# The last two raw weight chunks are converted inside the hand-over from attention to the expert, and VectorE splits the first weights

## The chip, the cores and the metric

One Trainium2 core runs the whole program. The metric is the device time in microseconds (us). The engines are TensorE (PE in the profile, with its weight loads as PEld), VectorE (DVE), ScalarE (ACT), GpSimd (POOL) and SyncE (SP), which issues every transfer of this kernel from one queue, in program order.

## The reference, cut to what matters

```python
scores = scale * q @ k.T                    # 4 batches x 12 heads, 448 tokens, head size 64
attn = softmax(where(mask, -1e9, scores)) @ v
x = attn.transpose(0, 2, 1, 3).reshape(1792, 768)
h = x @ w_in                                # w_in 768 x 2048, 64-bit floats in memory
P = a0 + a1*h + a2*h**2 + a3*h**3
Q = 1 + |b0|*|h| + |b1|*h**2
out = (P / (Q + 1e-6)) @ w_out              # w_out 2048 x 768, 64-bit floats in memory
```

## The kernel before, in words

**Attention.** The 48 heads are worked as 24 pairs, numbered p = 0 to 23. One pass of the loop over p is written out by hand in the string `ORDER`: each word is a task, and `@n` says for which pair it runs (`c.1@2` in pass p is the transposes of pair p-2). In a pass, TensorE transposes q and k (`psA`), multiplies scores (`psS`), transposes the normalized exponentials (`psC`) and multiplies with v (`psD`). VectorE adds the mask and takes the maxima (L329), ScalarE takes the exponentials (L339), GpSimd adds up the sums (`sm`, L346), VectorE inverts them (`r`, L349), GpSimd multiplies seven tiles by them (`n`, L353), and VectorE and ScalarE copy the transposes out of PSUM (`v`, `a`).

**Weights.** Each of the 32 blocks of 128 rows or columns of the weights ("chunk" m) arrives as 64-bit words (`raw`, 768 KB, `conv_load`) and is turned into 32-bit floats in steps: step 1 and step 5 are one GpSimd multiply each (L162, L166), step 2 and step 3 are one VectorE shift-and-or each (L172, L178), and the result (384 KB) is stored to memory (`conv_store`). There are three `raw` buffers, so chunk m+3 can be loaded when chunk m is done. The first ten chunks are converted in the attention passes: `quota(p)` says how many of the 20 half-chunks pass p takes. In the expert part each 32-bit block is loaded again (`load_w`, tag `ld`, three buffers used in turn) and split into a high part (`w_hi`, a rounding copy) and a low part (`w_lo`, a subtraction); a first-use block of `w_out` is stored split (L218).

**Expert.** Unit t is a block of 128 hidden features for 512 tokens: `p1(t)` are 18 products into `psH`, then a chain over ScalarE and VectorE (`act_a`, `dve_a`, `act_b`, `dve_b`) gives g, which is split into `gh` (ScalarE) and `gl`; `p2(t)` are 24 products into `psO` and `psM`.

**The hand-over.** After pass 23 the string `TAIL` orders the last attention tasks among the first expert tasks (`p1.0` to `p1.2`, `p2.0`); then a loop runs units t = 2 and on. Three facts of the code matter below. SP issues in program order, so a load that waits for a free `ld` buffer holds all behind it. `lw.4.0` takes the buffer that `wl.0.1` frees, `lw.2.1` the one that `wl.3.0` frees. And in the loop ScalarE makes `w_hi(2, 1)`, which reads what `lw.2.1` loaded, before its part `act_b(2)` of the chain:

```python
            if not late:
                split_w(t, 1)
            ...
            act_b(t)
```

In the names of the rows, `whl` is a split weight, `w` a 32-bit weight (or a scratch tile of the chain), `u` the scratch of a conversion (or of the chain).

Of the kernel before, what the change touches and what calls it, by code (L numbers as in the profile page):

```python
# [32 lines left out]
THIRD = "qk@-1 qy@-1 qx@-1" + ORDER.replace("qk@-1", "").replace(" qy@-1", "").replace(" qx@-1", "")  # L33

TAIL = """
c.1@2 e.6@1 c.0@2 e.0@1 v.1@2 dh@3 a.1@2 sm@1 v.0@2 a.0@2 r@1 dl@3 n.2@1 n.3@1 xr n.5@1 n.0@1 wh.1.0 p1.0 n.4@1
n.6@1 d@2 n.1@1 wl.1.0 c.1@1 c.0@1 co aa.0 da.0 dh@2 dl@2 a.1@1 v.1@1 dz.0 a.0@1 v.0@1 p1.1 wh.2.0 ab.0 wl.2.0 db.0 d@1 dy.0
lw.4.0 gh.0 gl.0 wh.0.1 wl.0.1 aa.1 da.1 p1.2 xl dh@1 dl@1 dz.1 ab.1 wh.1.1 wl.1.1 wh.3.0 lw.2.1 xa.10 p2.0
lw.3.1 aa.2 lw.5.0 db.1 wl.3.0 dy.1 wh.4.0 wl.4.0
"""  # L40

# [17 lines left out]
def kernel(  # L59
# [11 lines left out]
    nc = tc.nc  # L71
# [9 lines left out]
    NP = B * HP  # L81
# [18 lines left out]
    ab = const.tile([P, 6], F32, name="ab")  # L100
# [10 lines left out]
    xs = {  # L111
        (ck, part, kh): xp.tile([P, K3, 512], F32R, tag=f"x{ck}{part}{kh}", name="xs")
        for ck in range(2) for part in range(2) for kh in range(2)
    }
    x_raw = [xp.tile([P, K3, 2 * NT], F32, name=f"xr{kh}") for kh in range(2)]
    xr = {(kh, tk): x_raw[kh][:, :, tk * NT:(tk + 1) * NT] for kh in range(2) for tk in range(2)}
# [14 lines left out]
    def splits(t, n):  # L131


        return n == 0 or n_use[t] == 0
# [5 lines left out]
    def conv_load(m):  # L140
        if m >= len(items):
            return
        f, n = items[m]
        raw = c_raw[m] = cv.tile([P, DM, 2], U32, tag="raw", bufs=NR, name="raw64")
        if n == 0:
            nc.sync.dma_start(
                out=raw.rearrange("p (c f) t -> p c (f t)", c=KD),
                in_=moe_w_in[:, f * P:(f + 1) * P].bitcast(U32).rearrange("(c p) f -> p c f", p=P),
            )
        else:  # L150
            nc.sync.dma_start(
                out=raw.rearrange("p m t -> p (m t)"), in_=moe_w_out[f * P:(f + 1) * P, :].bitcast(U32)
            )

    def conv_step(m, s):
        raw = c_raw[m]
        yu = raw[:, :, 1]
        y = yu.bitcast(F32)
        if s == 1:
            pool, tag, bufs = (lv, f"u{m}", 1) if NL <= m < NC - 3 else (cv, "u", 3)  # L160
            u = c_u[m] = pool.tile([P, DM], U32, tag=tag, bufs=bufs, name="u")
            nc.gpsimd.tensor_scalar(  # L162
                out=u.bitcast(F32), in0=y, scalar1=0.0, scalar2=1.0, op0=ALU.mult, op1=ALU.mult
            )
        elif s == 5:
            nc.gpsimd.tensor_scalar(  # L166
                out=y, in0=y, scalar1=2.0 ** -112, scalar2=1.0, op0=ALU.mult, op1=ALU.mult
            )
        elif s == 4:
            nc.scalar.activation(out=y, in_=y, func=AF.Copy, scale=2.0 ** -112)  # L170
        elif s == 2:
            nc.vector.scalar_tensor_tensor(  # L172
                out=c_u[m], in0=raw[:, :, 0], scalar=29, in1=c_u[m],
                op0=ALU.logical_shift_right, op1=ALU.bitwise_or,
            )
        else:
            o = cv.tile([P, DM], F32, tag="ld", bufs=NL, name="w").bitcast(U32) if m < NL else c_u[m]
            nc.vector.scalar_tensor_tensor(  # L178
                out=o, in0=yu, scalar=3, in1=c_u[m], op0=ALU.logical_shift_left, op1=ALU.bitwise_or
            )  # L180
            c_32[m] = o.bitcast(F32)

    def conv_store(m):
        nc.sync.dma_start(out=w32[items[m]], in_=c_32[m])
        stored.add(items[m])

    def load_w(t, n):
        if t >= len(w_units) or (n_use[t] == 0 and (w_units[t][1], n) in items[:NL]):
            return
        f = w_units[t][1]  # L190
        if not splits(t, n):
            x = int(t < NPL + KF - 1 or (t - NPL - KF + 1) % 5 > 1)
            w = wp.tile([P, 2, DM], F32R, tag=f"w{x}", bufs=NWB[x], name="whl")
            nc.sync.dma_start(out=w.bitcast(F32), in_=w_hl[f, n])
            w_split[t, n] = (w[:, 0], w[:, 1])
        elif (f, n) in stored:
            w = cv.tile([P, DM], F32, tag="ld", bufs=NL, name="w")
            nc.sync.dma_start(out=w, in_=w32[f, n])
            w_raw[t, n] = w

    def w_hi(t, n):
        if not splits(t, n):
            return

        src = w_raw.pop((t, n)) if (t, n) in w_raw else c_32[items.index((w_units[t][1], n))]
        w = wp.tile([P, 2, DM], F32R, tag=f"w{n}", bufs=NWB[n], name="whl")
        nc.scalar.copy(out=w[:, 0], in_=src)
        w_split[t, n] = (w, src)

    def w_lo(t, n):  # L210
        if not splits(t, n):
            return
        w, src = w_split[t, n]
        eng = nc.gpsimd if t < 3 or n == 1 else nc.vector
        eng.tensor_tensor(out=w[:, 1], in0=src, in1=w[:, 0].bitcast(F32), op=ALU.subtract)  # L215
        w_split[t, n] = (w[:, 0], w[:, 1])
        if n == 1:
            nc.sync.dma_start(out=w_hl[w_units[t][1], n], in_=w.bitcast(F32))  # L218

    def split_w(t, n):  # L220
        w_hi(t, n)
        w_lo(t, n)
# [43 lines left out]
    def half(j):  # L266
        return slice(j * D, (j + 1) * D)
# [158 lines left out]
                nc.vector.tensor_copy(out=o, in_=ps[:, r])  # L426

    def quota(p):
        return int(3 <= p < NP - 1)

    steps = [(m, n) for m in range(NC) for n in (2, 3)]
    done = []
# [1 line left out]
    def conv(p, part):  # L434
        if part == 0:
            lo = sum(quota(x) for x in range(p))
            for m, n in steps[lo:lo + quota(p)]:
                conv_step(m, 1 if n == 2 else 5)
        elif part == 3:
            while done:  # L440
                conv_load(done.pop(0) + NR)
        else:
            lo = sum(quota(x) for x in range(p))
            mid, hi = lo + quota(p) // 2, lo + quota(p)
            for m, n in steps[lo:mid] if part == 1 else steps[mid:hi]:
                conv_step(m, n)
                if n == 3:
                    done.append(m)
# [391 lines left out]
    def coeffs():  # L840
        nc.sync.dma_start(out=ab[:, 0:4], in_=moe_a.partition_broadcast(P))
        nc.sync.dma_start(out=ab[:, 4:6], in_=moe_b.partition_broadcast(P))

    def coeffs_done():
# [4 lines left out]
    tasks.update({  # L849
        "co": coeffs_done, "xr": close_r, "xl": close_l, "p1": p1, "p2": p2, "aa": act_a, "da": dve_a, "dz": dve_a3,  # L850
        "ab": act_b, "db": dve_b, "dy": dve_b3, "gh": g_hi, "gl": g_lo, "wh": w_hi, "wl": w_lo,
        "lw": load_w, "xa": lambda m: conv_step(m, 1), "xs": conv_store, "xd": conv_load,
    })

    def evict_now():
# [24 lines left out]
    with tc.manual_schedule():  # L880
# [9 lines left out]
        sm = es_l.enter_context(pool(name="sm", bufs=4))  # L890
# [10 lines left out]
        for x in range(2):  # L901
            m = mask[half(x), S - QB:]
            nc.gpsimd.affine_select(
                out=m, in_=m, compare_op=ALU.is_ge, fill=-1e9 / SCALE, base=0, pattern=[[-1, QB]], channel_multiplier=1,
# [29 lines left out]
        def attend(p, part):  # L934
            for fn, arg, lag in part:
                if 0 <= p - lag < NP:
                    fn(p - lag, *arg)

        for p in range(NHEAD, NP):
            if p == 20:  # L940
                coeffs()
            if p in (1, 2, 3):
                conv_load((1, 2, 3).index(p))
            attend(p, begin[p] if 0 <= p < 3 else plan)
            for m in {20: (3, 0), 21: (4, 1, 5), 22: (6, 2, 7), 23: (8, 9)}.get(p, ()):
                conv_store(m)
            if p == NP - 2:
                split_w(0, 0)
            if p == NP - 2:
                load_w(0, 1)  # L950
            if p == NP - 1:
                load_w(3, 0)
                load_w(1, 1)
# [61 lines left out]
        for j in range(HF):  # L1015
            n = j + 5
# [46 lines left out]
```

## Time and profile before

| what | value |
|---|---|
| device time, median of 3 runs | 606.29 us (605.68 to 607.68) |
| the profiled execution's own time | 605.96 us |
| its span | 604.2 us |
| busy share of the span: PE, DVE, ACT, POOL | 98%, 88%, 74%, 30% |
| bytes moved | 131.00 MB, mean 217 GB/s |

The span is from the first to the last instruction; 1.76 us lie around it. Times in rows are counted from the span's start. A busy engine is one with an instruction in flight, which on VectorE and GpSimd holds time in which the instruction only stands; the idle time in brackets is that in front of an instruction, with what ended it.

### The profile page before, as it was taken

What the parts mean: (1) busy time and instruction counts of PE and PEld (TensorE: products, weight loads), DVE (VectorE), ACT (ScalarE), POOL (GpSimd) and SP (SyncE); (2) the same over time, 40 slices, a digit from 0 to 9 for tenths busy, and PEclk for the clock granted to TensorE, in tenths of its full rate; (3) what the DMA queues carried; (4) which work ended last, traced back from release to release, by engine and by line L of the source; (5) the groups of instructions that cost most, each with busy time, mean ns of one, the idle gap of its engine ahead of it and who ended that gap; (6) DMA issues with size and microseconds to landing.
All of it is one profiled execution on the core that took longest, in us unless ns stands there. A gap on an engine that the chain in (4) does not pass through costs nothing.

```text
span 604.2 us, 12764 instructions
## 1 busy us (share of the span) xinstructions
PE 594.9 (98%) x4660; PEld 494.6 (82%) x4660; DVE 534.7 (88%) x1013; ACT 446.4 (74%) x917; POOL 180.1 (30%) x274
## 2 busy tenths in 40 slices
PE   8999999999999999999999999999999999999997
PEld 6666666667788888888888888889999999998886
DVE  3999999985789999999999879998999999988950
ACT  4999999997687766777877776675486777677731
POOL 2899999886535311221333100000000000000000
PEclk9999999999999999999999999999999999999999
DMA  7979889788569988888985664433363343259872
GB/s 164 218 185 224 196 206 208 168 248 292 187 237 319 324 307 312 307 304 303 351 311 184 219 231 153 158 131 131 116 221 119 122 156 135 75 177 347 293 251 81
DMA packets 105727, 131.00 MB, mean 217 GB/s; under 512 B 70592, under 2 KB 83008, under 8 KB 105664
## 3 DMA queue, kind: packets, MB, share of 16 engines
q1 hardware_dynamic: 105664, 130.18, 68.0%
q8 instruction: 37, 0.61, 0.4%
q14 instruction: 26, 0.21, 0.1%
HBM read 99.49 MB, written 30.67 MB: 215 GB/s over the span
## 4 chain that ended last, share of the span: by engine, by line
PE 69%; DVE 15%; ACT 7%; issue 4%; POOL 4%; DMA 1%; SPq 0%; DVEq 0%; POOLq 0%; ACTq 0%
PE psO L601 22%; PE psH L232 17%; PE psQ L715 14%; PE psM L597 12%; ACT e L339 4%; DVE psS L329 4%; POOL e L353 3%; DVE at L384 3%; DVE u L172 2%; ACT at L382 1%; PE psS L318 1%; POOL whl L215 1%; PE psI L930 1%; DVE nm L329 1%; PE psC L372 1%
## 5 line engine op out<-in xcount | busy, mean ns | idle before, releaser
L601 PE MATMUL psO<-whl,gh 128*128 128x512 f32 x448 | 159.4, 392 | 0.3 <-ACT gh L527 0.2
L232 PE MATMUL psH<-xs,whl 128*128 128x512 f32 x576 | 136.7, 391 | 0.2 <-ACT e L339 0.2
L597 PE MATMUL psM<-whl,gh 128*128 128x256 f32 x448 | 126.3, 282 | 0.0
L232 PEld LDWEIGHTS psH<-xs,whl 128*128 128x128 f32 x576 | 106.0, 188 | 21.8 <-ACT e L339 0.3
L601 PEld LDWEIGHTS psO<-whl,gh 128*128 128x128 f32 x448 | 84.0, 188 | 18.7 <-ACT gh L527 1.5
L597 PEld LDWEIGHTS psM<-whl,gh 128*128 128x128 f32 x448 | 84.7, 189 | 1.6 <-DVE osb L585 0.3
L339 ACT ACTIVATE e<-psS,nm 128x448 f32<-128x448 f32 (+6 forms) x168 | 79.4, 571 | 5.8 <-DVE nm L329 3.7
L353 POOL TENSOR_SCALAR e<-e,r 128x192 f32<-128x192 f32 (+6 forms) x168 | 79.0, 492 | 11.4 <-DVE r L349 8.3
L601 PE MATMUL psO<-whl,gl 128*128 128x512 f32 x224 | 81.1, 391 | 0.0
L715 PE MATMUL psQ<-xpart,wq 128*128 128x384 f32 x432 | 78.5, 337 | 0.1
L715 PEld LDWEIGHTS psQ<-xpart,wq 128*128 128x128 f32 x432 | 74.7, 188 | 1.5 <-DVE hpair L741 0.4
L329 DVE CUSTOM_DVE_ANT_0 psS<-psS,mask 128x64 f32<-128x64 f32 (+6 forms) x168 | 65.5, 461 | 2.0 <-PE psS L318 1.3
L597 PE MATMUL psM<-whl,gl 128*128 128x256 f32 x224 | 63.2, 282 | 0.0
L162 POOL TENSOR_SCALAR u<-raw 128x768 f32<-128x768 f32 x32 | 39.2, 1226 | 53.8 <-DMA raw<-in_moe_w_out_dram 16.3
L318 PE MATMUL psS<-qkt 64*64 64x64 f32 (+6 forms) x672 | 47.5, 391 | 1.8 <-ACT e L339 1.6
L601 PEld LDWEIGHTS psO<-whl,gl 128*128 128x128 f32 x224 | 42.0, 188 | 8.8
L339 ACT ACTIVATION_READ_ACCUMULATOR e<-psS,nm 128x1 f32 x168 | 49.0, 303 | 0.0
L504 ACT ACTIVATE w<-w 128x512 f32<-128x512 f32 x32 | 20.2, 633 | 38.4 <-DVE w L489 38.3
L396 PE MATMUL psD<-at,vraw 128*64 128x448 f32 (+3 forms) x384 | 46.8, 386 | 0.4 <-issue 0.4
L396 PEld LDWEIGHTS psD<-at,vraw 128*64 128x64 f32 x384 | 25.6, 136 | 25.2 <-issue 14.7
L597 PEld LDWEIGHTS psM<-whl,gl 128*128 128x128 f32 x224 | 42.4, 189 | 0.0
L318 PEld LDWEIGHTS psS<-qkt 64*64 64x64 f32 x672 | 21.4, 132 | 20.8 <-ACT at L382 10.1
(109 smaller groups left out, 1119.2 us busy)
## 6 DMA issues: line engine op xcount, KB each, us to landing
whl<-whl SPq DMA_DIRECT2D x64, 768.0 KB, 5.3
w<-w SPq DMA_DIRECT2D x54, 384.0 KB, 5.0
raw<-in_moe_w_in_dram SPq DMA_DIRECT2D x16, 768.0 KB, 6.1
raw<-in_moe_w_out_dram SPq DMA_DIRECT2D x16, 768.0 KB, 5.6
w<-u SPq DMA_DIRECT2D x29, 384.0 KB, 3.1
qraw<-in_q_dram SPq DMA_DIRECT2D x48, 112.0 KB, 3.9
kraw<-in_k_dram SPq DMA_DIRECT2D x48, 112.0 KB, 3.9
out_dram<-osb SPq DMA_DIRECT2D x13, 384.0 KB, 3.1
```

Source lines behind the costliest of these rows:

```text
L162: nc.gpsimd.tensor_scalar(out=u.bitcast(F32), in0=y, scalar1=0.0, scalar2=1.0, op0=ALU.mult, op1=ALU.mult)
L232: nc.tensor.matmul(ps, w[:, c * P:(c + 1) * P], xs[ck, part, c // K3][:, c % K3], start=(c == 0 and n == 0), stop=(c == KD - 1 and n == 2),)
L318: nc.tensor.matmul(pss[p, b][half((1 + b + j) % 2)], QK[p][half(j), 0, b * QB:(b + 1) * QB], QK[p][half(j), 1, :b_w[b]], start=True, stop= ...
L329: nc.vector.tensor_tensor_reduce(out=s, in0=s, in1=mask[:, S - w:], scale=-SCALE, scalar=3e38, op0=ALU.add, op1=ALU.min, accum_out=nmx[p][ ...
L339: nc.scalar.activation(out=E[p % 2][i][:, :w], in_=pss[p, i], func=AF.Exp, bias=nmx[p][:, i:i + 1], scale=-1.0, accum_out=SUM[p % 2][:, i: ...
L353: nc.gpsimd.tensor_scalar(out=e, in0=e, scalar1=REC[p][:, i:i + 1], scalar2=0.0, op0=ALU.mult, op1=ALU.add)
L384: nc.vector.tensor_copy(out=o, in_=i)
L396: nc.tensor.matmul(ps[half(j), lo * QB:S], v[:, j, c], a[h][:, slot * QB:(slot + 7 - lo) * QB], start=(c == 0), stop=(c == 3), skip_group_ ...
L504: nc.scalar.activation(out=w, in_=w, func=AF.Abs)
L597: nc.tensor.matmul(acc["m", k], g, w[:, 512:], start=first and (k % 2 == 0 or each), stop=last, skip_group_check=True)
L601: nc.tensor.matmul(acc[k], g, w[:, :512], start=first, stop=last)
L715: nc.tensor.matmul(q_bank[j, bank], w[:, wp_, c * P:(c + 1) * P], xp_[:, c], start=(first and n == 0), stop=(n == 3 * K3 - 1), skip_group_ ...
```

## The change

Chunks 8 and 9 leave passes 19 to 22 (`quota` ends four passes sooner) and their steps, stores and the loads of chunks 11 and 12 are written into `TAIL`. The stores of pass 23 go with them. The split of unit 0's two blocks leaves ScalarE: both high parts become a VectorE copy, and the low part of the first block becomes a VectorE subtraction that stands in `TAIL` as `wl.0.0` (it was a GpSimd subtraction in pass 22). The coefficients' task `co` stands earlier.

```diff
 TAIL = """
-c.1@2 e.6@1 c.0@2 e.0@1 v.1@2 dh@3 a.1@2 sm@1 v.0@2 a.0@2 r@1 dl@3 n.2@1 n.3@1 xr n.5@1 n.0@1 wh.1.0 p1.0 n.4@1
-n.6@1 d@2 n.1@1 wl.1.0 c.1@1 c.0@1 co aa.0 da.0 dh@2 dl@2 a.1@1 v.1@1 dz.0 a.0@1 v.0@1 p1.1 wh.2.0 ab.0 wl.2.0 db.0 d@1 dy.0
-lw.4.0 gh.0 gl.0 wh.0.1 wl.0.1 aa.1 da.1 p1.2 xl dh@1 dl@1 dz.1 ab.1 wh.1.1 wl.1.1 wh.3.0 lw.2.1 xa.10 p2.0
+c.1@2 e.6@1 c.0@2 e.0@1 v.1@2 dh@3 a.1@2 xa.8 sm@1 xa.9 v.0@2 a.0@2 r@1 wl.0.0 co
+xc.8.2 xc.9.2 dl@3 n.2@1 n.3@1 xr n.5@1 n.0@1 wh.1.0 p1.0 n.4@1
+n.6@1 d@2 n.1@1 xc.8.5 xc.9.5 wl.1.0 c.1@1 c.0@1 aa.0 da.0 dh@2 dl@2 a.1@1 v.1@1 dz.0 a.0@1 v.0@1 xc.8.3 xs.8 xd.11
+p1.1 wh.2.0 ab.0 wl.2.0 db.0 d@1 dy.0
+lw.4.0 xc.9.3 xs.9 xd.12 gh.0 gl.0 wh.0.1 wl.0.1 aa.1 da.1 p1.2 xl dh@1 dl@1 dz.1 ab.1 wh.1.1 wl.1.1 wh.3.0 lw.2.1 xa.10 p2.0
 lw.3.1 aa.2 lw.5.0 db.1 wl.3.0 dy.1 wh.4.0 wl.4.0
 """
...
-        nc.scalar.copy(out=w[:, 0], in_=src)
+        if t:
+            nc.scalar.copy(out=w[:, 0], in_=src)
+        else:
+            nc.vector.tensor_copy(out=w[:, 0], in_=src)
...
-        eng = nc.gpsimd if t < 3 or n == 1 else nc.vector
+        eng = nc.gpsimd if 0 < t < 3 or n == 1 else nc.vector
...
     def quota(p):
-        return int(3 <= p < NP - 1)
+        return int(3 <= p < NP - 5)
...
-        "lw": load_w, "xa": lambda m: conv_step(m, 1), "xs": conv_store, "xd": conv_load,
+        "lw": load_w, "xa": lambda m: conv_step(m, 1), "xc": conv_step, "xs": conv_store, "xd": conv_load,
...
-            for m in {20: (3, 0), 21: (4, 1, 5), 22: (6, 2, 7), 23: (8, 9)}.get(p, ()):
+            for m in {20: (3, 0), 21: (4, 1, 5), 22: (6, 2, 7)}.get(p, ()):
                 conv_store(m)
             if p == NP - 2:
-                split_w(0, 0)
-            if p == NP - 2:
+                w_hi(0, 0)
                 load_w(0, 1)
```

On SP, from the end of pass 22 into the hand-over, before (`raw_3224` is chunk 12, `w_5_0` and `w_3_1` are the stores of chunks 8 and 9, `w<-w_4_0` is `lw.4.0`, `w<-w_2_1` is `lw.2.1`):

```order
119 L198 DMA w<-w_0_1_84 128x768
120 L146 DMA raw_3224<-in_moe_w_in_dram 128x6x256
121 L184 DMA w_5_0_93<-u 128x768
122 L184 DMA w_3_1_90<-u 128x768
123 L198 DMA w<-w_3_0_89 128x768
124 L198 DMA w<-w_1_1_86 128x768
125 L198 DMA w<-w_4_0_91 128x768
126 L218 DMA whl_1_115<-whl 128x1536
127 L218 DMA whl_1_116<-whl 128x1536
128 L198 DMA w<-w_2_1_88 128x768
```

The same place on SP in the change (`raw_3434` is now chunk 11, `raw_3477` chunk 12):

```order
118 L200 DMA w<-w_0_1_84 128x768
119 L200 DMA w<-w_3_0_89 128x768
120 L200 DMA w<-w_1_1_86 128x768
121 L186 DMA w_5_0_93<-u 128x768
122 L153 DMA raw_3434<-in_moe_w_out_dram 128x1536
123 L200 DMA w<-w_4_0_91 128x768
124 L186 DMA w_3_1_90<-u 128x768
125 L148 DMA raw_3477<-in_moe_w_in_dram 128x6x256
126 L223 DMA whl_1_115<-whl 128x1536
127 L223 DMA whl_1_116<-whl 128x1536
128 L200 DMA w<-w_2_1_88 128x768
```

Two stores and two loads of raw chunks moved behind loads that wait for buffers; one store (chunk 9) and one raw load (chunk 12) now stand between `lw.4.0` and `lw.2.1`.

On VectorE, the hand-over before, from the last reciprocal to the chain of unit 1:

```order
440 L349 RECIPROCAL r<-r 128x7
441 L845 TENSOR_SCALAR na<-ab 128x4
442 L489 SCALAR_TENSOR_TENSOR w<-w,bb,psH 128x512
...
447 L384 COPY at<-psC 128x8x64
448 L512 SCALAR_TENSOR_TENSOR w<-w,u 128x512
449 L515 SCALAR_TENSOR_TENSOR p<-p,na,u 128x512
450 L521 SCALAR_TENSOR_TENSOR p<-w,p 128x512
451 L489 SCALAR_TENSOR_TENSOR w<-w,bb,psH 128x512
```

The same place on VectorE in the change:

```order
437 L354 RECIPROCAL r<-r 128x7
438 L220 TENSOR_TENSOR whl<-w,whl 128x768
439 L850 TENSOR_SCALAR na<-ab 128x4
440 L174 SCALAR_TENSOR_TENSOR u<-raw_2201,u 128x768
441 L174 SCALAR_TENSOR_TENSOR u<-raw_2466,u 128x768
442 L494 SCALAR_TENSOR_TENSOR w<-w,bb,psH 128x512
...
448 L180 SCALAR_TENSOR_TENSOR u<-raw_2201,u 128x768
449 L517 SCALAR_TENSOR_TENSOR w<-w,u 128x512
...
451 L526 SCALAR_TENSOR_TENSOR p<-w,p 128x512
452 L180 SCALAR_TENSOR_TENSOR u<-raw_2466,u 128x768
453 L212 CAST whl<-w 128x768
454 L494 SCALAR_TENSOR_TENSOR w<-w,bb,psH 128x512
```

Six instructions of 768 elements came in among the chain of units 0 and 1: `wl.0.0`, steps 2 and 3 of both chunks, and the high part of unit 0's second block.

## Rows read from the trace of the kernel before

**Rows 1.** The page's first line.

```profile
span 604.2 us, 12764 instructions
```

**Rows 2.** Waits of TensorE, 105 to 420 us: for whom, us in total, times, longest.

```profile
PE psC L372 <- POOL e L353: 0.7, 3, 0.3
...
PE psO L601 <- ACT gh L527: 0.2, 1, 0.2
```

**Rows 3.** Timeline of TensorE, start of three passes' transposes: start us, us, instruction.

```profile
116.73 0.41 PE L286 MATMUL psA<-ident,qraw 64*128 64x64 f32 x8
...
122.55 0.41 PE L286 MATMUL psA<-ident,qraw 64*128 64x64 f32 x8
...
127.94 0.41 PE L286 MATMUL psA<-ident,qraw 64*128 64x64 f32 x8
```

**Rows 4.** Timeline of VectorE, passes 20 and 23 and the hand-over.

```profile
120.80 0.97 DVE L178 SCALAR_TENSOR_TENSOR u<-raw,u 128x768 uint32<-128x768 uint32 x1
...
135.46 0.20 DVE L349 RECIPROCAL r<-r 128x7 f32<-128x7 f32 x1 [0.99 <-POOL r L346]
...
145.90 0.75 DVE L489 SCALAR_TENSOR_TENSOR w<-w,bb,psH 128x512 f32<-128x512 f32 x1 [5.08 <-ACT p L484]
...
150.84 0.69 DVE L512 SCALAR_TENSOR_TENSOR w<-w,u 128x512 f32<-128x512 f32 x1 [1.21 <-ACT u L508]
...
155.60 0.75 DVE L489 SCALAR_TENSOR_TENSOR w<-w,bb,psH 128x512 f32<-128x512 f32 x1 [2.67 <-ACT p L484]
...
160.02 2.42 DVE L215 TENSOR_TENSOR whl<-w,whl 128x768 fp32r<-128x768 f32 x1
```

**Rows 5.** Timeline of GpSimd, passes 20 to 22 and the hand-over.

```profile
118.04 3.97 POOL L353 TENSOR_SCALAR e<-e,r 128x192 f32<-128x192 f32 x7 [0.41 <-DVE xs L424]
121.98 0.92 POOL L162 TENSOR_SCALAR u<-raw 128x768 f32<-128x768 f32 x1
...
133.31 1.82 POOL L215 TENSOR_TENSOR whl<-w,whl 128x768 fp32r<-128x768 f32 x1 [0.85 <-ACT whl L207]
...
159.33 2.30 POOL L215 TENSOR_TENSOR whl<-w,whl 128x768 fp32r<-128x768 f32 x1 [2.56 <-ACT whl L207]
```

**Rows 6.** The chain of work that ended last, 136 to 232 us, two pieces.

```profile
162.07 4.55 DMA w<-w
166.65 0.84 ACT whl L207
```

**Rows 7.** Waits of VectorE, 165 to 232 us; then busy times, 170 to 223 us.

```profile
DVE w L512 <- ACT u L508: 2.1, 1, 2.1
...
170.00:223.00 53.00, 52.75 (x267) 44.78 (x266) 52.65 (x70) 40.79 (x61) 18.89 (x14) 1.00 0.87 312
```

**Rows 8.** Timeline of SP's queue: start of issue, us, transfer, in two stretches.

```profile
156.79 0.32 SPq L198 DMA_DIRECT2D w<-w  x1
...
205.94 0.32 SPq L184 DMA_DIRECT2D w<-u  x1
206.35 0.39 SPq L146 DMA_DIRECT2D raw<-in_moe_w_in_dram  x1
...
209.87 0.32 SPq L218 DMA_DIRECT2D whl<-whl  x1
210.24 0.42 SPq L198 DMA_DIRECT2D w<-w  x1
```

**Rows 9.** The same five transfers, one window each: size, us from issue to landing.

```profile
w<-w SPq DMA_DIRECT2D x1, 384.0 KB, 3.6
...
w<-u SPq DMA_DIRECT2D x1, 384.0 KB, 2.7
...
raw<-in_moe_w_in_dram SPq DMA_DIRECT2D x1, 768.0 KB, 5.3
...
whl<-whl SPq DMA_DIRECT2D x1, 768.0 KB, 5.7
...
w<-w SPq DMA_DIRECT2D x1, 384.0 KB, 6.3
```

## The prediction

> **What bounds the kernel now.** I read the waits of TensorE first. The span is 604.2 us [rows 1], and between 105 and 420 us TensorE waits for GpSimd's normalized exponentials three times, 0.7 us in all, and once, for 0.2 us, for `gh` of an expert unit [rows 2]. The reader should see how little that is: TensorE sets the pace nearly everywhere, so a gain counts only if it survives up to the places where something else sets it.
>
> Then I read who makes TensorE wait. Around pass 20 the passes start at 116.73, 122.55 and 127.94 us [rows 3], so that one took 5.82 us and the next 5.39. In the longer one GpSimd's seven multiplications took 3.97 us [rows 5], and their end lies in the 0.97 us of VectorE's step 3 of chunk 8 [rows 4]. In pass 23 the reciprocal waits 0.99 us for the sums [rows 4], which stand behind GpSimd's subtraction of the first weights, 133.31 to 135.13 [rows 5].
>
> Last I read the chain that ended last, in the expert's first units. It does not run through TensorE there: it goes through the load `lw.2.1`, issued at 162.07 and 4.55 us under way, to ScalarE's high part of that block at 166.65 [rows 6]. ScalarE makes it ahead of `act_b(2)`, so VectorE, which needs `act_b(2)`, waits 2.1 us; after that VectorE is busy 52.65 of 53.00 us from 170 to 223 [rows 7], and the one wait of TensorE for `gh` [rows 2] falls into this stretch. So whatever delays the landing of `lw.2.1` delays a VectorE that has no idle time to catch up with, and TensorE behind it. A gain before that landing is kept only if this landing moves forward too.
>
> **The change part by part.**
>
> *Passes 19 to 22.* They lose four VectorE steps (0.97 us, row at 120.80) and four GpSimd multiplies (0.92 us alone, row at 121.98) [rows 4, 5]. TensorE's floor for a pass is the undisturbed 5.39 us, so pass 19, which was not disturbed, gains nothing, and pass 20 gains 5.82 - 5.39 = 0.43 us. ScalarE loses the first high part; VectorE gets it as a copy of 768 elements where a step of 0.97 us stood in pass 22, and I cost it at nothing: it takes the place of that step. If the copy took longer than the step it would push VectorE's copies of `psC`.
>
> *Pass 23.* GpSimd's subtraction is gone from in front of the sums, so the reciprocal's wait of 0.99 us goes, and with it maxima and exponentials move up, behind which `p1.0` starts. Together `p1.0` starts 0.43 + 0.99 = 1.4 us sooner.
>
> *The hand-over, VectorE and GpSimd.* VectorE gets six instructions of 768 elements (`wl.0.0`, four steps, one copy), by the same row 0.97 us each, 5.8 us; it was idle there 5.08, 1.21 and 2.67 us, 9.0 in all [rows 4]. GpSimd gets four multiplies of 0.92 us, 3.7 us, and loses one subtraction; SP's waits apart, nobody waits for them directly. So the work has room, but its order has not. When GpSimd's subtraction started at 159.33 and VectorE's at 160.02, VectorE's took 2.42 us and ended only after GpSimd's at 161.63 [rows 4, 5], 1.45 us more than the 0.97 of a two-source step. New neighbours of this kind are: chunk 8's step 3 and then `db.0` beside `wl.1.0` and `wl.2.0`, and the copy of `wh.0.1` beside `gl.0`; `gh.0`, `gl.0` and `wl.0.1` come behind them. With no such collision this little chain moves up with `p1.0`, by 1.4 us; with one it stays, with two it is 1.5 us late. I take +0.5 us, between one and two, nearer to one, since part of the second is covered by the 2.67 us of idle time.
>
> The Trainium skill says why in "SBUF — State Buffer", section "Who interferes with whom": a VectorE instruction with two inputs in SBUF, or a copy in its two-port mode, and a GpSimd instruction that reads SBUF exclude each other for a whole instruction, and the later one waits. The row pair agrees. By that rule alone, all three meetings cost their full length and the chain is nearer to 1.5 us late, 1.0 more than I take. The same notes, "VectorE: DVE Perf Modes", section "Mode 2×_2P — use both read ports for one tensor", let a copy of 32-bit floats run at two elements a cycle, an estimate of 0.4 us for this one; no run shows it yet, and by it the chain would be some 0.5 us sooner.
>
> *The hand-over, SP's queue.* This is the part that I expect to decide. SP issues in order. The store of chunk 9 and the load of chunk 12, which were issued in pass 23, now stand behind `lw.4.0`, which waits for the buffer that `wl.0.1` frees, and in front of two stores of split weights and of `lw.2.1`. What such transfers cost in a row I take from five issued together later [rows 8, 9]. The store of 384 KB issued at 205.94 landed at 208.64, the load of a raw `w_in` chunk issued at 206.35 at 211.65: 3.0 us behind it. The store of 768 KB issued at 209.87 landed at 215.57, the 384 KB load issued at 210.24 at 216.54: 1.0 us behind it. So they land one after another, 1.0 us for 384 KB, by the same rate 1.95 for 768 KB, and 3.0 for a raw `w_in` chunk.
>
> Before, `lw.4.0` was issued at 156.79 and landed at 160.39 [rows 8, 9]. Two stores (3.9) and `lw.2.1` (1.0) back to back would end at 165.3; it landed at 162.07 + 4.55 = 166.6 [rows 6]. So the queue had 1.3 us to spare. The two new transfers take 1.0 + 3.0 = 4.0 us, and 4.0 - 1.3 = 2.7 us are left over; with `lw.4.0` issued 0.5 us later, `lw.2.1` lands 3.2 us later, near 169.8. The ends: with `lw.4.0` 1.4 us sooner 1.3 us, with it 1.5 us later 4.2 us. The other two transfers moved (store of chunk 8, load of chunk 11) are issued behind `lw.1.1` and ahead of `lw.4.0`, and SP stands still for `lw.4.0` anyway; I cost them at nothing, and if they ran into `lw.4.0` they would cost up to 1.0 + 1.95 us.
>
> *Sum.* The 1.4 us at `p1.0` are not kept: VectorE sets the pace from 170 to 223 us, and it starts when `lw.2.1` has landed. The shift of the end is the shift of that landing, +3.2 us. The profiled execution took 605.96 us, so 609.2; the median of the runs stands 0.33 us above it, so 609.5 us in the terms of that median. Its own range is 607.6 to 610.5.
>
> **The rivals.** A change within 0.3% (1.8 us) is about what a measurement of this kernel cannot tell from none; faster thus means below 604.5 us, slower above 608.1.
>
> *The transfers are hidden.* If the queue takes the store and the raw load beside the others, or the 1.3 us to spare are really more, `lw.2.1` lands when it did, and only the little chain's collisions count: about 0, 606.3 us, between 605.7 and 607.2. For it: SP's stretch before had free time, and the raw load is read from memory while the stores write to it. Against it: the five transfers of rows 8 and 9 landed one behind another.
>
> *The gain is carried.* This is the case on the other side. If no VectorE instruction meets one of GpSimd's, `wl.0.1` and `wl.3.0` end 1.4 us sooner, and if the queue is also empty then, `lw.2.1` lands before 165.2 us and the whole expert moves up: 606.29 - 1.4 = 604.9 us. It decides only if both hold, and 160.02's row speaks against the first.
>
> *TensorE's clock falls.* Under my forecast TensorE stands still once for 3 to 4.5 us: it is 1.4 us early, and `gh.2` is 3.2 us late. The granted clock was 1.00, the upper level of 2.4 GHz, through all of 170 to 223 us [rows 7], where it waited 0.2 us at most; no row here shows it after a wait of 4 us. If it is granted 1.2 GHz for as long as it stood, it loses half of that time, 1.5 to 2.2 us: about 609.5 + 1.8 = 611.3 us. The Trainium skill, "TensorE: Matmul & The Clock Gate", section "What's actually happening", has an idle TensorE fall to the lower level and come back when busy.
>
> **How the numbers follow.** The forecast 0.62, hidden 0.20, carried 0.10, clock 0.08. The range from 605.6 to 610.5 leaves out the carried gain and the clock's fall, 0.18 together; the likeliest case has 607.6 to 610.5. Slower by over 0.3%: the clock's 0.08 and 0.87 of the forecast's 0.62, together 0.62. Faster: half of the carried case (its 604.9 is close to the bound) and a little of hidden, 0.07. Within: 0.31.
>
> **What would show it.** Right: `psC` in pass 21 without its wait for GpSimd; the reciprocal in pass 23 without one; `p1.0` 1.4 us sooner; `lw.2.1` issued near 162 and landed near 170; VectorE's wait ahead of `act_b(2)`'s products some 3 us longer; one wait of TensorE for `gh` of 3 to 4.5 us soon after that landing; everything behind about 3 us later. Wrong: the landing of `lw.2.1` within 1 us of 166.6, or VectorE with idle time between 170 and 223 us, which would give the delay back.

## The result, and the profile after

The change is slower: 609.99 us median of 6 runs (608.40 to 611.03) against 605.64 of 6 runs of the kernel before; the ratio is 1.0064, its 95% interval 1.0045 to 1.0083. The forecast was 609.5. The profiled execution took 610.16 us, 608.3 of them its span.

The waits of TensorE, 105 to 420 us, answer to [rows 2]:

```profile
PE psO L606 <- ACT gh L532: 4.3, 1, 4.3
PE psC L377 <- POOL e L358: 0.2, 1, 0.2
```

What the change was to remove is gone: `psC` waits once for 0.2 us, where it waited three times. In its place stands one wait of 4.3 us for `gh`.

The start of the three passes of [rows 3], then TensorE's first expert products and those around the wait (timeline: start us, us, instruction; in brackets the idle time in front and what ended it):

```profile
115.77 0.41 PE L291 MATMUL psA<-ident,qraw 64*128 64x64 f32 x8
...
121.16 0.41 PE L291 MATMUL psA<-ident,qraw 64*128 64x64 f32 x8
...
126.55 0.41 PE L291 MATMUL psA<-ident,qraw 64*128 64x64 f32 x8
...
137.41 4.40 PE L237 MATMUL psH<-xs,whl 128*128 128x512 f32 x18 [0.18 <-ACT e L344]
...
167.82 4.25 PE L237 MATMUL psH<-xs,whl 128*128 128x512 f32 x18
...
176.37 0.79 PE L606 MATMUL psO<-whl,gh 128*128 128x512 f32 x1 [4.30 <-ACT gh L532]
...
183.29 4.29 PE L237 MATMUL psH<-xs,whl 128*128 128x512 f32 x18
...
187.42 0.39 PE L606 MATMUL psO<-whl,gh 128*128 128x512 f32 x1
...
191.58 4.26 PE L237 MATMUL psH<-xs,whl 128*128 128x512 f32 x18
...
203.94 0.39 PE L606 MATMUL psO<-whl,gh 128*128 128x512 f32 x1
```

In the kernel before, `p1.0` started here:

```profile
140.00 4.40 PE L232 MATMUL psH<-xs,whl 128*128 128x512 f32 x18 [0.18 <-ACT e L339]
```

So `p1.0` is 2.59 us sooner, and three parts make that up. At 115.77 this execution is already 0.96 us ahead of 116.73 [rows 3]. That is a difference of two executions and no gain: a lead of 0.98 us is there in the program's first 11 us (the second row of this kind starts at 9.37 against 10.35), and pass 19, the only earlier one that the change touches, takes 5.38 us against 5.40. Pass 20 takes 5.39 us instead of 5.82, 0.43. From the start of pass 22 to `p1.0` it takes 10.86 us instead of 12.06, 1.20.

VectorE and GpSimd, the places of [rows 4, 5]:

```profile
130.72 0.75 DVE L212 CAST whl<-w 128x768 fp32r<-128x768 f32 x1
...
146.96 3.29 DVE L180 SCALAR_TENSOR_TENSOR u<-raw,u 128x768 uint32<-128x768 uint32 x1
...
153.03 1.66 DVE L212 CAST whl<-w 128x768 fp32r<-128x768 f32 x1
...
159.02 2.42 DVE L220 TENSOR_TENSOR whl<-w,whl 128x768 fp32r<-128x768 f32 x1
```

```profile
117.07 3.20 POOL L358 TENSOR_SCALAR e<-e,r 128x192 f32<-128x192 f32 x7 [0.94 <-DVE xs L429]
...
127.85 3.20 POOL L358 TENSOR_SCALAR e<-e,r 128x192 f32<-128x192 f32 x7 [0.91 <-DVE r L354]
...
145.78 3.65 POOL L220 TENSOR_TENSOR whl<-w,whl 128x768 fp32r<-128x768 f32 x2
...
152.98 1.29 POOL L539 TENSOR_TENSOR gl<-p,gh 128x512 fp32r<-128x512 f32 x1 [3.54 <-ACT gh L532]
```

The seven multiplications of pass 20 (117.07) take 3.20 us where they took 3.97 [rows 5]. In the hand-over the new steps do meet. Step 3 of chunk 8 is in flight from 146.96 to 150.25 and ends 0.82 us behind the second of GpSimd's two subtractions, which end at 149.43. The copy of `wh.0.1` takes 1.66 us and ends 0.42 us behind `gl.0` (152.98 + 1.29 = 154.27). The other copy, in pass 22, took 0.75 us; it too ends 0.42 us behind GpSimd's multiplications (127.85 + 3.20 = 131.05).

SP's queue and the chain that ended last, the places of [rows 6, 8]:

```profile
156.66 0.32 SPq L200 DMA_DIRECT2D w<-w  x1
157.03 0.42 SPq L186 DMA_DIRECT2D w<-u  x1
157.50 0.42 SPq L148 DMA_DIRECT2D raw<-in_moe_w_in_dram  x1
157.97 3.00 SPq L223 DMA_DIRECT2D whl<-whl  x2
161.01 1.92 SPq L200 DMA_DIRECT2D w<-w  x2
```

```profile
161.01 8.36 DMA w<-w
169.40 0.83 ACT whl L210
```

`lw.2.1` was issued 1.06 us sooner than before and landed 2.75 us later: 8.36 us under way instead of 4.55 [rows 6]. It lands 12.7 us behind the issue of `lw.4.0`, before 9.9. Behind it VectorE waits (waits 165 to 232 us, and its busy time from 170 to 223, as in [rows 7]):

```profile
DVE w L517 <- ACT u L513: 5.8, 1, 5.8
```

```profile
170.00:223.00 53.00, 50.37 (x64) 0.94 0.84 300
```

The wait of 2.1 us has become 5.8. The granted clock of this stretch is no longer 1.00 but 0.94; by windows of 5 us (length, TensorE's busy time and instructions, granted clock, share of the DMA engines, GB/s):

```profile
170.00:175.00 5.00, 2.07 (x10) 1.00 0.40 166
175.00:180.00 5.00, 3.63 (x11) 0.53 0.72 254
180.00:185.00 5.00, 5.00 (x22) 0.79 0.68 237
185.00:190.00 5.00, 5.00 (x27) 1.00 0.71 264
```

TensorE stands from 172.07 (167.82 + 4.25) on. In shorter windows the clock is at its upper level of 2.4 GHz up to about 175.3, falls to the lower level of 1.2 GHz while TensorE still stands, and is back at about 182.1, behind nearly 6 us of products. `p2(2)`, 176.37 to 183.29, takes 6.92 us; the next unit's 24 products take 4.16 (187.42 to 191.58).

### The profile page after: what moved, and what is told of

Its sections match the earlier page's. It is cut to its first block, busy times and chain, and to the rows that moved or that the text cites. A ratio compares the mean times of both kernels' runs of the same rounds, so it can differ in the third digit from the quotient of the medians.

```text
span 608.3 us, 12767 instructions
## 1 busy us (share of the span) xinstructions
PE 596.4 (98%) x4660; PEld 495.4 (81%) x4660; DVE 540.3 (89%) x1016; ACT 445.0 (73%) x915; POOL 175.3 (29%) x273
## 4 chain that ended last, share of the span: by engine, by line
PE 87%; POOL 4%; DVE 3%; issue 2%; ACT 2%; DMA 1%; SPq 0%; POOLq 0%; DVEq 0%; ACTq 0%
PE psO L606 24%; PE psH L237 19%; PE psQ L720 14%; PE psM L602 13%; PE psS L323 6%; PE psD L401 6%; PE psC L377 4%; POOL e L358 2%; PE psA L291 2%; DMA w<-w 1%; POOL whl L220 1%; PE psI L935 1%; ACT e L344 1%; DVE psS L334 1%; DVE at L389 0%
## 5 line engine op out<-in xcount | busy, mean ns | idle before, releaser
L606 PE MATMUL psO<-whl,gh 128*128 128x512 f32 x448 | 161.5, 396 | 4.3 <-ACT gh L532 4.3
L358 POOL TENSOR_SCALAR e<-e,r 128x192 f32<-128x192 f32 (+6 forms) x168 | 80.4, 501 | 13.0 <-DVE r L354 9.7
L164 POOL TENSOR_SCALAR u<-raw 128x768 f32<-128x768 f32 x32 | 36.3, 1133 | 58.1 <-DMA raw<-in_moe_w_in_dram 23.4
```

Source lines behind the costliest of these rows:

```text
L164: nc.gpsimd.tensor_scalar(out=u.bitcast(F32), in0=y, scalar1=0.0, scalar2=1.0, op0=ALU.mult, op1=ALU.mult)
L358: nc.gpsimd.tensor_scalar(out=e, in0=e, scalar1=REC[p][:, i:i + 1], scalar2=0.0, op0=ALU.mult, op1=ALU.add)
L606: nc.tensor.matmul(acc[k], g, w[:, :512], start=first, stop=last)
```

## The experiments

The theory was that of the forecast: the two transfers put in front of `lw.2.1` delay its landing, VectorE has no time to make that good, and all of it reaches the end; beside it, that the clock's fall after TensorE's wait costs more. The rivals: VectorE's six new instructions and their meetings with GpSimd are the cause; the slow products are hidden; a short queue is a gain whatever the change does. Ratios are to runs of the kernel before on the same chip.

**a1_behind**, both transfers behind `lw.2.1`:

```diff
-lw.4.0 xc.9.3 xs.9 xd.12 gh.0 gl.0 ... wh.3.0 lw.2.1 xa.10 p2.0
-lw.3.1 aa.2 lw.5.0 db.1
+lw.4.0 xc.9.3 gh.0 gl.0 ... wh.3.0 lw.2.1 xs.9 xa.10 p2.0
+lw.3.1 aa.2 lw.5.0 xd.12 db.1
```

> The change, with the store of chunk 9 and the load of chunk 12 put behind lw.2.1 in SP's queue. Theory (queue): lw.2.1 is still issued near 161 us and lands near 166 instead of 169.4; ScalarE's wait for it falls from 6.0 to about 2 us, VectorE's wait ahead of the unit-2 products from 5.8 to about 2, TensorE's wait for gh from 4.3 to under 1; the granted clock stays at 1.00 and the time is that of the kernel before or a little less, 605.0 us (604.3 to 606.0). Rival (six more VectorE instructions and their meetings with GpSimd are the cause): the queue matters little, 609 to 610.

Measured: 607.04 us, ratio 1.0026 (1.0012 to 1.0041). The landing came as expected, and the time did not. ScalarE's high parts (timeline) and two pieces of the chain that ended last:

```profile
166.45 0.83 ACT L210 CAST whl<-w 128x768 fp32r<-128x768 f32 x1 [2.92 <-DMA w<-w]
...
173.25 0.83 ACT L210 CAST whl<-w 128x768 fp32r<-128x768 f32 x1 [1.88 <-DMA w<-w]
```

```profile
161.67 6.95 DMA w<-u
169.11 4.12 DMA w<-w
```

The first wait is mended. The second is new: `lw.3.1` reads what chunk 9's store wrote, so it was issued only when that store had landed, 6.95 us after its own issue, and `lw.5.0`, behind it in the queue, landed at 173.2. ScalarE, which makes that high part ahead of `gh` of unit 2, stood for it. TensorE waited 2.25 us, and in this execution the clock held:

```profile
174.65 0.50 PE L606 MATMUL psO<-whl,gh 128*128 128x512 f32 x1 [2.25 <-ACT gh L532]
```

```profile
175.00:180.00 5.00, 5.00 (x29) 1.00 1.04 424
```

So VectorE's new work is not the cause of most of the loss, since it is all in this kernel; but where the store goes matters as much as where the raw load goes.

**b1_queue_alone**, the kernel before with only the two transfers moved:

```diff
-lw.4.0 gh.0 gl.0 wh.0.1
+lw.4.0 xs.9 xd.12 gh.0 gl.0 wh.0.1
...
-23: (8, 9)
+23: (8,)
...
-                conv_load(done.pop(0) + NR)
+                m = done.pop(0) + NR
+                if m != 12:
+                    conv_load(m)
```

> The kernel before, with nothing changed but the place of two transfers: the store of chunk 9 and the load of chunk 12 leave pass 23 and stand between lw.4.0 and lw.2.1. Theory (queue): lw.2.1 lands 2.7 us later, near 169.3; gh of unit 2 is 2.7 later and TensorE waits about 2 us for it; 2.5 us slower than before, 608.1, and if the clock falls after so short a wait too, up to 2 us more. Rival (VectorE's work is the cause): no difference from before, 605.6.

Measured: 608.89 us, ratio 1.0058 (1.0045 to 1.0071). With nothing of the change but these two transfers, most of the loss is there. ScalarE's wait for `lw.2.1`, TensorE's for `gh`, and the clock in 175 to 180 us:

```profile
169.14 0.84 ACT L207 CAST whl<-w 128x768 fp32r<-128x768 f32 x1 [5.06 <-DMA w<-w]
```

```profile
176.14 0.50 PE L603 MATMUL psO<-whl,gh 128*128 128x512 f32 x1 [2.00 <-ACT gh L529]
```

```profile
175.00:180.00 5.00, 3.86 (x14) 0.70 0.77 273
```

In this execution the clock fell with a wait of 2.00 us, in that of a1_behind it did not with one of 2.25. Their other executions do not differ so: the mean granted clock of the whole span is 0.997 in this profiled one, as in three more of the five runs here and in five of the seven of a1_behind, and 0.999 or more in the rest.

**a2_fill**, more products in TensorE's wait:

```diff
         wih, wil = w_split.pop((t, 0))
+        for c in range(16 * (t == 4)):
+            nc.tensor.matmul(
+                ps, wih[:, c % KD * P:(c % KD + 1) * P], xs[ck, 0, c % KD // K3][:, c % KD % K3], start=c == 0, stop=c == 15
+            )
```

> The change, with 16 more products into psH ahead of p1(4), overwritten by it, so that TensorE works through most of its 4.3 us wait for gh of unit 2. Theory (the queue delays the landing by 2.7 us, and the clock's fall after the wait costs another 1.7): granted clock 1.00 in 175 to 185 us, p2(2) takes 4.2 us instead of 6.9, and the kernel is 1.7 us faster than the change, 608.3, though it does 3.8 us more of products. Rival (the slow products are hidden behind VectorE's late chain): no difference from the change, 610.0; or, if TensorE has no free time there, 3.8 us slower.

Measured: 609.13 us, ratio 1.0067 (1.0054 to 1.0080), no clear difference from the change on another chip, while its profiled execution had the clock at 1.00 and took 608.43. So the same kernel was run beside the change on one chip, later.

**c_change** and **c_fill**:

> The change itself, on the chip on which c_fill runs. Both theories: 1.0064 times before, about 609.7.

> The change with 16 more products into psH ahead of p1(4), overwritten by it, the same kernel as a2_fill, on one chip with the change, since a2_fill's median and its trace did not agree on the size. Theory (the clock's fall costs 1.7 us): 1.5 to 1.9 us faster than c_change. Rival (0.9 or less, as the medians of different chips had it): 0.9 us faster or less.

Measured: the change 609.91 us, ratio 1.0069 (1.0053 to 1.0086); with the products 609.10, ratio 1.0060 (1.0042 to 1.0077). Over all their runs the medians are 609.98 (12 of the change) and 609.13 (11 with the products). The profile of c_fill, clock by window, and where TensorE meets VectorE's chain again:

```profile
175.00:180.00 5.00, 4.28 (x24) 1.00 0.76 273
```

```profile
201.99 0.50 PE L610 MATMUL psO<-whl,gh 128*128 128x512 f32 x1 [0.65 <-ACT gh L536]
```

With TensorE at work the clock does not fall, and 3.8 us of further products make nothing slower. In these profiled executions `p2(5)` starts at 201.99 in c_fill and at 204.00 in c_change, and the times are 608.30 and 610.18. Not all of that is the clock's, since `lw.2.1` itself came 0.81 us later in c_change. ScalarE's high part of its block, in c_change and c_fill:

```profile
169.94 0.84 ACT L210 CAST whl<-w 128x768 fp32r<-128x768 f32 x1 [6.95 <-DMA w<-w]
```

```profile
169.13 0.84 ACT L210 CAST whl<-w 128x768 fp32r<-128x768 f32 x1 [6.04 <-DMA w<-w]
```

From the start of that high part to the end of the span it is 437.4 us in c_fill and in a2_fill, 438.5 in c_change and 438.9 in the first profile of the change (spans of 606.5, 606.6, 608.4 and 608.3 us). So behind the landing the clock's fall costs 1.1 to 1.5 us in these executions, between the theory and the rival. The medians give 0.8, on the rival's side, but the runs overlap (608.40 to 611.33 and 608.01 to 610.97), so that the medians alone do not show it.

**a3_stores_late**, as a1_behind, with the two stores of split weights behind `lw.2.1` too (`ws.t` issues the store of block t that `wl.t.1` issued):

```diff
-wh.3.0 lw.2.1 xs.9 xa.10
+wh.3.0 lw.2.1 ws.0 ws.1 xs.9 xa.10
```

> As a1_behind, and the two stores of split weights (768 KB each, blocks 0 and 1 of w_out) also put behind lw.2.1, so that nothing is under way ahead of it on the queue. Theory (transfers of this queue land one behind another): lw.2.1, issued near 161, lands near 163.5; VectorE's 2 us wait for unit 2 goes, TensorE keeps the time that it is ahead; 1.5 us faster than before, 604.1. Rival (a load takes 4.5 us there whatever stands ahead of it): as a1_behind.

Measured: 609.69 us, ratio 1.0070 (1.0056 to 1.0084), a miss: 604.1 had been expected. ScalarE's high parts:

```profile
165.16 0.84 ACT L210 CAST whl<-w 128x768 fp32r<-128x768 f32 x1 [1.15 <-DMA w<-w]
...
175.40 0.83 ACT L210 CAST whl<-w 128x768 fp32r<-128x768 f32 x1 [5.29 <-DMA w<-w]
```

`lw.2.1` landed by 165.2, but chunk 9's store now stood behind 1.5 MB, and the load that reads it made ScalarE stand 5.29 us. What was seen in a1_behind, larger.

**a5_load_behind**, **a6_store_behind**, **a8_load_later**: one transfer moved at a time.

```diff
 a5  lw.4.0 xc.9.3 xs.9 gh.0 ... lw.3.1 aa.2 lw.5.0 xd.12 db.1
 a6  lw.4.0 xc.9.3 xd.12 gh.0 ... wh.3.0 lw.2.1 xs.9 xa.10
 a8  lw.4.0 xc.9.3 xs.9 gh.0 ...   and in the loop of units, behind load_w(t + 2, 1):
+            if t == 2:
+                conv_load(12)
```

> The change, with the load of chunk 12 alone put behind lw.5.0 on SP's queue; the store of chunk 9 stays behind lw.4.0. Theory (the raw load is 3.0 of the 4.0 us that stand in the way, the store's 1.0 fits into the 1.3 us that the queue had to spare, and no load waits for its own store): lw.2.1 lands near 166.5 us, lw.3.1 and lw.5.0 do not come late, TensorE's wait for gh stays under 1 us at a clock of 1.00; 605.2 us, within 0.8 of before. Rival (VectorE's six more instructions cost something of their own): 607 or more with that landing in time.

> The change, with the store of chunk 9 alone put behind lw.2.1; the load of chunk 12 stays behind lw.4.0. Theory (raw load 3.0 us, less 1.3 to spare): lw.2.1 lands near 168.3, 1.7 us late; after it lw.3.1 waits for the store that it reads, as in a1_behind, where that cost a second wait, so lw.5.0 lands near 175 and ScalarE stands for it; 608.5 to 610. Rival (the raw load is read beside the others and costs nothing): lw.2.1 near 166.4 and the time of a1_behind, 607.0.

> As a5_load_behind, but the load of chunk 12 is issued only after unit 2's transfers, near 176 us, so that no raw load is under way while lw.2.1, lw.3.1 and lw.5.0 are read; the store of chunk 9 stays behind lw.4.0. In a5_load_behind lw.2.1 came 11.5 us after the issue of lw.4.0, against 9.8 before. Theory (the raw load issued 3 us behind lw.2.1 takes its turns from it): lw.2.1 comes 9.8 to 10.3 after lw.4.0, TensorE's wait is about 1 us, 605.5 to 606. Rival (the store of chunk 9 costs 1.7 us there, and the queue had nothing to spare): 11.5 again, and 607 to 608.

Measured: a5 607.97 us, ratio 1.0036 (1.0022 to 1.0049); a6 609.17, 1.0059 (1.0047 to 1.0072); a8 607.61, 1.0033 (1.0016 to 1.0049). The times of a5 and a8 miss the theory (605.2, and 605.5 to 606); a6 is inside its 608.5 to 610, though `lw.2.1` landed near 169.4 and not 168.3. ScalarE's wait for `lw.2.1` in the three, in this order:

```profile
169.31 0.84 ACT L210 CAST whl<-w 128x768 fp32r<-128x768 f32 x1 [4.83 <-DMA w<-w]
```

```profile
169.38 0.83 ACT L210 CAST whl<-w 128x768 fp32r<-128x768 f32 x1 [5.59 <-DMA w<-w]
```

```profile
166.65 0.84 ACT L210 CAST whl<-w 128x768 fp32r<-128x768 f32 x1 [2.50 <-DMA w<-w]
```

Since the executions start up differently, the landing is best counted from the issue of `lw.4.0` (SP's row) to the start of that high part:

| transfers between `lw.4.0` and `lw.2.1` | kernels | us |
|---|---|---|
| chunk 9's store alone | a7_loads_first | 7.2 |
| none | b3_loads_first, a3_stores_late | 8.0, 7.9 |
| two stores of split weights | before, a1 | 9.9, 9.6 |
| these two and chunk 9's store | a8; a5 (raw load behind `lw.5.0`) | 9.2; 11.6 |
| these two and the raw load of chunk 12 | a6 | 12.3 |
| these two, chunk 9's store and the raw load | change, c_change, a2_fill, c_fill, a4, b1 | 12.7, 13.7, 12.6, 12.8, 12.9, 12.7 |

In these executions, one for each kernel, the raw load costs some 2.5 us (a6 against before and a1) and the store nothing (a8). The store's nothing fits the 1.3 us to spare; the raw load's 2.5 does not, since by that count 3.0 - 1.3 = 1.7 us were expected. How firm such a price is, the change and c_change show: they are one kernel and differ by 0.9 us. In a5 the store was not alone: the raw load, issued 2.9 us behind `lw.2.1` (162.18 and 165.09 in SP's rows), was under way when it landed, and in a8, without that, it landed 2.3 us sooner. a8's profiled execution took 605.95 us, inside the theory's range. But its 12 runs spread from 605.65 to 610.26, and the median is the rival's; the four longest, 608.15 and more, had a mean granted clock of 0.994 to 0.997, the other eight 0.999 and more. So the clock fell in those four and not in the profiled one, and what made them longer no profile shows. With chunk 9's store as the one addition in the way the median is 2.2 us above before (605.44), so that the store costs nothing is shown for the profiled execution alone. Whether a load behind `lw.2.1` delays it is therefore open: two profiled executions say so, the medians hardly tell a5 from a8.

**a4_split_back**, the change with unit 0's split on ScalarE and GpSimd:

```diff
-        if t:
-            nc.scalar.copy(out=w[:, 0], in_=src)
-        else:
-            nc.vector.tensor_copy(out=w[:, 0], in_=src)
+        nc.scalar.copy(out=w[:, 0], in_=src)
...
-        eng = nc.gpsimd if 0 < t < 3 or n == 1 else nc.vector
+        eng = nc.gpsimd if t < 3 or n == 1 else nc.vector
...
-                w_hi(0, 0)
+                split_w(0, 0)
```

(and `wl.0.0` is taken out of `TAIL`.)

> The change, with the split of unit 0's two blocks back on ScalarE and GpSimd as before. Theory (the queue decides): p1.0 starts about 1 us later, since the reciprocal of pass 23 waits for GpSimd again; lw.4.0 no later, lw.2.1 lands as late as in the change or up to 1 us later; TensorE is less far ahead, so its wait for gh is 3 to 4 us and the time stays at 610.0, within 0.7. Rival (VectorE's share of the split is what delays the chain): 1 to 2 us faster than the change.

Measured: 610.84 us, ratio 1.0091 (1.0069 to 1.0112), 0.8 above the theory and not faster as the rival had it. The reciprocal of pass 23 waits again, and `p1.0`:

```profile
134.90 0.20 DVE L351 RECIPROCAL r<-r 128x7 f32<-128x7 f32 x1 [1.11 <-POOL r L348]
```

```profile
139.44 4.38 PE L234 MATMUL psH<-xs,whl 128*128 128x512 f32 x18 [0.19 <-ACT e L341]
```

From the start of its pass 22 at 127.37 to `p1.0` it is 12.07 us, against 10.86 in the change and 12.06 before: VectorE's split is worth 1.2 us there, and is not what makes the change slow.

**a7_loads_first** and **b3_loads_first**: the stores of split weights behind the three loads, in the change (with chunk 12's load behind them too) and in the kernel before.

```diff
 a7  lw.4.0 xc.9.3 xs.9 gh.0 ... wh.3.0 lw.2.1 xa.10 p2.0
     lw.3.1 aa.2 lw.5.0 ws.0 ws.1 xd.12 db.1
 b3  lw.4.0 gh.0 gl.0 ... lw.3.1 aa.2 lw.5.0 ws.0 ws.1 db.1
```

> As a5_load_behind, and the two stores of split weights (768 KB each) also behind lw.5.0, so that lw.4.0, the store of chunk 9, lw.2.1, lw.3.1 and lw.5.0 are the only transfers in that stretch. Theory: lw.2.1 lands near 165, as in a3_stores_late, and here the next two loads are not late either; VectorE's wait of 2 us for unit 2 goes, TensorE keeps the 1.4 us that it is ahead: 604.0 us. Rival (what TensorE is ahead is lost at a later wait anyway): 605.2, as a5_load_behind.

> The kernel before, with the two stores of split weights (768 KB each) behind lw.5.0, as in a7_loads_first, and nothing else. It tells whose gain that kernel's 1.0 us is. Theory (the change's attention part puts TensorE 1.6 us ahead, and the short queue only lets it keep that): here TensorE is not ahead and waits for gh 0.2 us at most, so lw.2.1 lands near 164.5 and nothing comes of it: 605.3, within 0.4 of before. Rival (the short queue is the gain): 604.5.

Measured: a7 604.55 us (11 runs), ratio 0.9983 (0.9973 to 0.9993), faster than both kernels; b3 605.13 us, ratio 0.9994 (0.9982 to 1.0005). ScalarE's wait for `lw.2.1` in a7, what is left of TensorE's waits there, and ScalarE's wait in b3:

```profile
165.00 0.84 ACT L210 CAST whl<-w 128x768 fp32r<-128x768 f32 x1 [0.43 <-DMA w<-w]
```

```profile
198.54 0.50 PE L613 MATMUL psO<-whl,gh 128*128 128x512 f32 x1 [0.47 <-ACT gh L539]
```

```profile
164.78 0.84 ACT L207 CAST whl<-w 128x768 fp32r<-128x768 f32 x1 [0.40 <-DMA w<-w]
```

The early landing alone brings no gain that can be measured; with the change's attention part the kernel is 1.0 us faster than before. The two intervals overlap, so that the attention part makes the difference is the theory's account, borne out by both medians and not shown beyond noise. In a7 TensorE is 1.6 us ahead at `p1.0` (138.61 against 140.00, though its pass 19 starts 0.25 us later than before) and pays 0.47 of it back at `gh` of unit 5. All six of VectorE's new instructions are in this kernel too, and it is faster than the one without them.

## Why the prediction was right, point by point

*Attention.* Right. Pass 20: 0.43 us expected, 0.43 measured. Pass 23: 0.99 expected from the reciprocal's wait, 1.20 measured; the reciprocal waits no more. One reading was inexact: the seven multiplications of before end at 122.01, 0.24 us behind step 3 and not inside it; that the two share its time holds, since without the step they take 3.20. The copy of pass 22 took 0.75 us, no longer than the step it replaces, and `psC` did not wait for it.

*The little chain.* Nearly right. `lw.4.0` was issued at 156.66 against 156.79 [rows 8]; set against the 0.96 us by which this execution was ahead, 0.8 us late, 0.5 expected. Two meetings came, at 146.96 and 153.03. The Trainium skill, "SBUF — State Buffer", section "Who interferes with whom", lets a VectorE instruction with two SBUF inputs stand while GpSimd reads there. The 3.29 us of the first agree. How many of GpSimd's instructions it stands through was open: two here, and one in c_change, where the same step took 1.48 us and ended before the second. The estimate of 0.4 us for a copy fits both copies, which end 0.42 us behind GpSimd; in pass 22 the gain from it was hidden by a meeting that the prediction had not named.

*The queue.* Right in its sum, 2.7 us: 12.74 instead of 9.86 us from `lw.4.0`'s issue, 2.9, and in b1_queue_alone, which has only this, 12.65. Of its parts the raw load alone cost 2.5 us where 3.0 - 1.3 = 1.7 had been counted, and the store alone nothing, as counted, in single profiled executions; so the sum came out better than its terms. The price of transfers in a row was also read from less than the text says: of the five transfers issued from 205.94 to 210.24, rows 8 and 9 show four, in two pairs, and leave out the 768 KB load issued between these at 206.83. That transfers land one behind another was enough for this sum; a5_load_behind and a8_load_later leave open whether it holds strictly. The other two transfers moved, costed at nothing, were issued at 150.28 and 150.65; `lw.4.0` landed 3.4 us behind its issue, 3.6 before [rows 9], and b1_queue_alone, which leaves them in place, has the same 12.65 us.

*All of it reaches the end.* Right. Against the start of pass 20, `lw.2.1` lands 2.75 + 0.96 = 3.7 us later, 3.2 expected, and with the clock held up by more products the kernel is 3.7 us slower than before on both chips (609.13 against 605.41, 609.10 against 605.44). From the start of ScalarE's high part of that block to the end of the span it is 437.6 us before and in a8, 437.4 in a2_fill and c_fill, 437.7 in a4 and a6, 437.9 in a5 and b1: with the landing anywhere from 166.65 to 170.38, the rest takes the same within some 0.5 us. One of the signs of being wrong came by the letter, VectorE idle for 2.63 us between 170 and 223; 2.31 of them are the end of its wait for that landing, up to 172.31, and give nothing back.

*The clock.* This step failed: the forecast and the clock's fall were set against each other as two cases, and both came. The fall had a chance of 0.08, because no row showed the clock after a wait of 4 us. `p2(2)` lost 6.92 - 4.16 = 2.8 us. Of that TensorE gets back what it would have waited for `gh` of unit 5 anyway: `p2(5)` starts at 203.94, and that `gh` ends at 201.54 + 0.62 = 202.16, so 1.8 us remain at that point in this execution. At the end of the span 1.1 to 1.5 remain in the two profiles of the change, by the same count 0.3 to 0.5 in a4, a5, a6 and b1, where the clock was at the lower level for a shorter time, and 0.8 in the medians of c_change and c_fill. The Trainium skill, "TensorE: Matmul & The Clock Gate", section "What's actually happening", has idleness bring the lower level and activity end it; the windows agree.

*The sum.* In part luck. The forecast was a shift of 3.2 us on a median of 606.29 from three runs; over six runs that median is 605.64, and the shift is 4.35. The base was 0.65 us too high and the shift 1.1 too small, 0.5 of it at the landing and the rest most likely at the clock, which the sum had at nothing; so 609.5 stands nearer to 609.99 than its working does.

*The rivals.* "Hidden" falls with the landing at 169.4, and with b1_queue_alone. "The gain is carried" needs an empty queue; a7_loads_first shows that case, 1.0 us under before, where 1.4 was worked out, although its VectorE does meet GpSimd (the same step takes 3.29 us).

## What to carry to other kernels

When a transfer is moved, count the loads behind it on its queue, the loads that read what it wrote, and its neighbours: here a raw load of 768 KB cost the needed load behind it 2.5 us in one profiled execution, and a store moved out of the way made the load of its own data late. A gain ahead of a wait is worth nothing until the wait itself moves; here the same 1.6 us of TensorE's lead were lost in the change and partly kept when only the order on SP's queue was mended. And where a forecast has TensorE standing for some us, its clock belongs into the sum and not beside it.

## What the runs showed of the hardware

- The clock fell with a wait of TensorE of 2.00 us (mean 0.70 in the window 175 to 180 us, b1_queue_alone), and held at 1.00 with 2.25 us (a1_behind); with 4.3 us the mean of that window was 0.53. The length of the wait alone does not decide it, and most other runs of a1_behind have the mean clock of runs with a fall. In the change it fell while TensorE stood; in b1_queue_alone and a5_load_behind it fell near 177.0 and 177.7 us, 0.9 and 1.4 us after the products had begun again (176.14 and 176.31). The Trainium skill, "TensorE: Matmul & The Clock Gate", section "What's actually happening", has the moment of the change vary from run to run; these runs fit that and do not prove it.
- A VectorE step that started at 146.96, while GpSimd's first subtraction was under way, ended at 150.25, behind the second, which followed the first without a gap. In c_change the same step, started at 146.74, ended at 148.22, between the two.
- A VectorE copy of 768 32-bit floats per partition took 0.75 us at 130.72 and 1.66 at 153.03; both ended 0.42 us after the GpSimd instructions under way beside them. The two-input steps and subtractions that met GpSimd ended 0.82 us after it (150.25 against 149.43, 161.44 against 160.62).
- A store of 384 KB took 6.95 us from issue to landing (a1_behind) with a 768 KB store issued before it still under way, and the load that reads it was issued only then.
